# Attention scores in 64x32 tiles of the array, with another layout of queries, values and weight conversion

## The chip, the cores and the metric

One core of a Trainium2 chip runs the whole program. The metric is device time in microseconds (us) of one execution, as the median of several runs. The engines are PE (TensorE: matmuls and transposes), DVE (VectorE), ACT (ScalarE), POOL (GpSimd) and SP (SyncE, which here issues all DMAs); 16 DMA engines move the data.

## The reference

Three stages follow one another. The attention has 4 batches, 8 heads, 512 local and 32 global positions and a head dimension of 64. Global queries see all 544 keys; a local query sees the 32 global keys and the local keys at a distance of at most 32. Then come two FFNs on 2176 tokens with 512 features and 2048 hidden units; all is float32.

```python
s_g = scale * q_g @ concat(k_g, k_l).T            ; out_g = softmax(s_g) @ concat(v_g, v_l)
s_l = scale * concat(q_l @ k_g.T, masked(q_l @ k_l.T, |i-j| <= 32)); out_l = softmax(s_l) @ concat(v_g, v_l)
x   = concat(out_g, out_l) as [2176, 512]
x   = relu(x @ w_in)**2 @ w_out                    # first FFN
y   = rational(x @ w_in2) @ w_out2                 # second FFN, P/Q with coefficients a, b
```

The four weight matrices arrive with 8 bytes an element and are converted on the chip to float32; for the matmuls of the FFNs each is split into a high and a low part.

## The kernel before, in words

**Attention.** The work goes by quads: a quad is one batch and four heads, eight quads in all, and a quad has five groups: four local groups of 128 queries (four blocks of 32) and one global group (g = 4). In a software pipeline (the loop at L747, 41 iterations) iteration i does the scores of group i+3 (`do_S`, L589), the exponentials of group i+2, the transposes of the probabilities of group i+1 (`do_T`, L649), the product with the values of group i (`do_PV`, L679) and the transposes of group i-2's results into `xT` (`do_xT`, L713). All engines issue in the order of the program text: it is a hand-written order, with semaphores put in by the framework. Where group i+2 is global, the scores of group i+3, the first of the next quad, are placed late, after `do_xT` (L772).

For the scores of a block of 32 queries, L602 multiplies a stationary matrix of 128 rows (two heads of 64 features) and 64 columns (the queries of one head, zeros, and the other way round: `qbd`, a block-diagonal layout) by 128 keys of a window (32 global, 96 local). Two such matmuls (four heads) fill the 128 partitions of a bank; a group has eight. They go to one bank of PSUM from tag "S", which has two buffers. DVE adds the mask, takes the minimum and so the row's maximum (L608), ACT takes the exponentials (L616). PV (L696) has 16 matmuls of 128 rows and 32 columns a group.

`prep` (L548) transposes the queries and keys of later quads: keys two quads ahead, queries one. For the keys, the 32 global ones are copied by DVE into six slots (L556). For the queries, four transposes of [128, 128] a pass and four copies by ACT (L577) that sort them into the block-diagonal layout. Two passes a quad.

The values of a quad stand in 14 windows of 128 rows (32 global, 96 local), of three kinds by where the global rows lie: A, B and C, interleaved in memory. `load_v(n, "A")` (part 0) loads the local rows of the five A windows and the global rows of one; `load_v(n, "B")` makes the rest by seven DMAs inside SBUF (L458 to L465). All DMAs stand in SP's one queue. The tuples `LD` and `LD0` say in which group of a quad which load is issued, `PZ` and `PZ0` in which group which pass of `prep` runs.

**Weight conversion.** `todo` is a list of items, half weight tiles (16 feature tiles f, a half each for w_in and w_out). `cv_tick` advances them: every third tick loads one item, and later ticks run its steps on ACT (L121, L131), DVE (L124, L135, L139), POOL (L129, L144) and for the ready value a copy and a subtraction (L153, L159). An item marked spill is instead written back to DRAM as float32 and loaded later, ready ("f32"), when only the last two steps remain. In attention there are 63 ticks (3 in the first iteration, then 2 and 1 in turn), so 21 items: 14 for f = 0 to 6, four spilled for f = 14 and 15, three more. The first FFN group (`step`, L356, for the first 16 k) runs 14 ticks in three steps for the rest, before the weights of each f are needed.

**FFNs.** `step(k)` does twelve matmuls into "S" for one f (L252) and twelve for the output of an earlier one (L328), with the squares and splits on ACT and DVE between them (L265 to L276).

## Time and profile before

| | |
|---|---|
| runs | 969.3, 967.54, 963.17 us; median 967.54 |
| profiled execution | 964.78 us, of which the profile's span is 963.0 |
| busy, share of the span | PE 96%, PEld (weight loads) 87%, DVE 75%, ACT 59%, POOL 38% |
| DMA | 81.82 MB; queue of SP 32.3% of 16 engines |

A profile shows, for one execution, when each engine ran which instruction, and for each idle time which event ended it. The share over the whole span is a mean over stages with different limits. In a timeline a row is start, duration, engine, line, operation, tiles and, in brackets, the idle time before it and what ended it. PE's durations overlap, as matmuls are pipelined: the time of a group is read from its start to the start of the next. The granted clock is 1.00 at 2.4 GHz and 0.50 at 1.2 GHz.

### The profile page before, as it was taken

The page shows a single profiled execution, that of the slowest core. Times are in us where ns is not written, and L with a number is a line of the kernel's source. Part 1 is how long each engine was busy: PE and PEld are TensorE (multiplying, and loading weights), DVE is VectorE, ACT ScalarE, POOL GpSimd, SP SyncE. Part 2 cuts the span into 40 slices and gives each one's busy share as a digit, 9 for nine tenths or more (in the row PEclk, how much of TensorE's full clock was granted, in tenths as well). Part 3 has the DMA queues.
Part 4 walks back from the last instruction along what each step waited for, and adds up shares of the span by engine and source line. Part 5 has one row for each costly group of instructions (what it writes and reads, how often), then busy time and mean ns, then how long its engine had stood idle before and what let it go on. Part 6 is the DMA issues. An engine that isn't in the chain of part 4 may idle for free.

```text
span 963.0 us, 18278 instructions
## 1 busy us (share of the span) xinstructions
PE 920.3 (96%) x6794; PEld 833.4 (87%) x6794; DVE 719.5 (75%) x1525; ACT 572.8 (59%) x1223; POOL 366.8 (38%) x349
## 2 busy tenths in 40 slices
PE   8899988999999999999999988899999999999996
PEld 5677766989999999999999977789989989989874
DVE  4586768798645674453334599999999999999996
ACT  4697877678434553443324476666766666666674
POOL 2143433343211221111000088755555555555553
PEclk9899999999999999999999999999999999999999
DMA  9899998355522433222002322000010010010000
GB/s 216 175 231 243 211 210 210 99 152 167 155 90 92 148 116 114 95 88 77 1 1 66 99 66 74 3 30 4 1 33 1 1 33 1 1 33 1 8 27 22
DMA packets 78121, 81.82 MB, mean 85 GB/s; under 512 B 24528, under 2 KB 64720, under 8 KB 78032
## 3 DMA queue, kind: packets, MB, share of 16 engines
q1 hardware_dynamic: 78032, 80.66, 32.3%
q8 instruction: 53, 0.87, 0.4%
q14 instruction: 36, 0.29, 0.1%
HBM read 56.36 MB, written 13.89 MB: 73 GB/s over the span
## 4 chain that ended last, share of the span: by engine, by line
PE 57%; issue 13%; DVE 12%; POOL 6%; DMA 5%; ACT 4%; SPq 2%; POOLq 0%; DVEq 0%; ACTq 0%
PE S L252 26%; PE T L328 5%; PE PV L331 5%; PE tr L331 4%; PE T L331 4%; PE PV L328 4%; PE tr L328 3%; DMA S<-in_moe_w_in_dram 3%; POOL w L159 2%; POOL big L308 2%; DVE ts L300 2%; PE S L602 2%; DVE w L159 1%; POOL tq L289 1%; DVE T L139 1%
## 5 line engine op out<-in xcount | busy, mean ns | idle before, releaser
L252 PE MATMUL S<-big,w 128*128 128x384 f32 (+1 forms) x2304 | 410.3, 327 | 0.9 <-ACT big L265 0.9
L252 PEld LDWEIGHTS S<-big,w 128*128 128x128 f32 x2304 | 385.9, 188 | 9.7 <-ACT big L265 1.2
L144 POOL TENSOR_TENSOR T<-T,S 128x512 uint32<-128x512 uint32 x64 | 87.5, 1367 | 292.4 <-DVE T L139 184.2
L289 POOL TENSOR_TENSOR tq<-tq,big 128x384 f32<-128x384 f32 (+1 forms) x96 | 93.4, 973 | 261.4 <-DVE tq L287 249.4
L273 DVE TENSOR_TENSOR big<-big 128x384 f32<-128x384 f32 (+1 forms) x80 | 46.4, 580 | 141.8 <-ACT big L269 141.6
L308 POOL TENSOR_TENSOR big<-ts,big 128x384 fp32r<-128x384 f32 (+1 forms) x96 | 124.5, 1297 | 5.2 <-issue 1.9
L300 DVE SCALAR_TENSOR_TENSOR ts<-ts,coef,big 128x384 f32<-128x384 f32 (+1 forms) x96 | 125.6, 1308 | 0.0
L265 ACT ACTIVATE big<-S 128x384 f32<-128x384 f32 (+1 forms) x96 | 45.4, 473 | 114.1 <-PE S L252 112.5
L286 ACT ACTIVATE big<-S 128x384 f32<-128x384 f32 (+1 forms) x96 | 45.5, 474 | 105.2 <-PE S L252 78.9
L331 PE MATMUL PV<-w,big 128*128 128x512 f32 x288 | 99.9, 401 | 3.7 <-ACT big L307 2.6
L331 PE MATMUL T<-w,big 128*128 128x512 f32 x288 | 84.1, 400 | 11.5 <-POOL big L308 10.8
L328 PE MATMUL T<-big,w 128*128 128x384 f32 x384 | 88.0, 337 | 2.0 <-DVE big L276 1.8
L269 ACT ACTIVATE big<-big 128x384 fp32r<-128x384 f32 (+1 forms) x96 | 48.8, 508 | 64.4 <-PE T L328 27.0
L328 PE MATMUL PV<-big,w 128*128 128x384 f32 (+1 forms) x384 | 82.2, 322 | 0.3 <-DVE xs L707 0.3
L328 PE MATMUL tr<-big,w 128*128 128x384 f32 (+1 forms) x384 | 82.0, 322 | 0.0
L288 ACT ACTIVATE ts<-S,coef 128x384 f32<-128x384 f32 (+1 forms) x96 | 62.7, 653 | 25.7 <-POOL big L308 25.0
L331 PEld LDWEIGHTS T<-w,big 128*128 128x128 f32 x288 | 52.0, 188 | 25.4 <-POOL big L308 17.5
L331 PE MATMUL tr<-w,big 128*128 128x512 f32 x240 | 71.5, 395 | 0.0
L328 PEld LDWEIGHTS T<-big,w 128*128 128x128 f32 x384 | 68.1, 188 | 3.9 <-DVE big L276 3.9
L331 PEld LDWEIGHTS PV<-w,big 128*128 128x128 f32 x288 | 52.5, 188 | 19.4 <-POOL big L308 7.5
L328 PEld LDWEIGHTS PV<-big,w 128*128 128x128 f32 x384 | 64.9, 188 | 0.6 <-issue 0.6
L328 PEld LDWEIGHTS tr<-big,w 128*128 128x128 f32 x384 | 64.8, 188 | 0.0
(137 smaller groups left out, 1430.2 us busy)
## 6 DMA issues: line engine op xcount, KB each, us to landing
S<-in_moe_w_out_dram SPq DMA_DIRECT2D x32, 512.0 KB, 4.0
scr<-T SPq DMA_DIRECT2D x36, 256.0 KB, 2.2
T<-scr SPq DMA_DIRECT2D x36, 256.0 KB, 2.7
S<-in_moe_w_in_dram SPq DMA_DIRECT2D x32, 256.0 KB, 5.5
S<-in_moe_w_in_dram SPq DMA_DIRECT2D x16, 512.0 KB, 3.9
out_dram<-xT SPq DMA_DIRECT2D x17, 256.0 KB, 2.6
kr<-in_k_l_dram SPq DMA_DIRECT2D x7, 512.0 KB, 8.2
qr<-in_q_l_dram SPq DMA_DIRECT2D x7, 512.0 KB, 6.1
```

Of the source, the lines that this page charges most:

```text
L144: gp.tensor_tensor(out=u, in0=u, in1=it["S"][:, :, 0], op=ALU.add)
L252: pe.matmul(h, wk[k][s], x[k][t], start=m == 0, stop=m == 3 * NK - 1)
L265: sc.activation(g, h, AF.Relu)
L269: sc.activation(hi, g, AF.Square)
L273: ve.tensor_tensor(out=g, in0=g, in1=g, op=ALU.mult)
L286: sc.activation(av, h, AF.Abs)
L288: sc.activation(s, h, AF.Identity, scale=coef[:, 3:4], bias=coef[:, 2:3])
L289: gp.tensor_tensor(out=q, in0=q, in1=av, op=ALU.mult)
L300: ve.scalar_tensor_tensor(out=s, in0=s, scalar=coef[:, 0:1], in1=r, op0=ALU.add, op1=ALU.mult)
L308: gp.tensor_tensor(out=lo, in0=s, in1=hi.bitcast(F32), op=ALU.subtract)
L328: pe.matmul(y[m][:, 0:n], a, x, start=st and z == 0, stop=sp and z == 2)
L331: pe.matmul(y[m], a, x, start=st and z == 0, stop=sp and z == 2)
```

## The change

Scores: a group's 16 matmuls now have 64 rows (one head) and 32 columns (one block); even heads of a pair go to one bank, odd ones to another, so a group takes two banks of "S". Each bank holds two blocks of two heads side by side, and the masks are made for pairs of blocks. Queries: a new `turn_q` has ACT copy a quad's raw queries from [head, c, d] to [c, head, d], after which four transposes a pass give two heads' queries by one copy; there are no zeros to set. Values: the windows of one kind lie side by side in memory (`win`); the global rows are loaded three times and spread by POOL; four DMAs inside SBUF remain. The global keys' slots are filled by POOL instead of DVE. The copy of the transposed probabilities of g = 3 goes from ACT to DVE. The loads of q and k move in `LD`. Weights: no items are spilled in attention; 14 items are loaded there, three more in the last five groups.

```diff
-    SPL = (14, 15)
     if wide:
-        todo += items(0, range(NPRE), "wide")
-        todo += items(0, SPL, "wide", True)
-        for f in range(NPRE, NF):
-            todo += items(0, (f,), "f32" if f in SPL else "wide")
+        todo += items(0, range(NF), "wide")
         todo += items(1, range(NF), "wide", True)
...
     todo.reverse()
+    later = len(todo) - 2 * NPRE
...
+        def win(x):
+            return 5 * (x % 3) + x // 3
...
-            A, Bw, C = wf[:, 0::3], wf[:, 1::3], wf[:, 2::3]
+            A, Bw, C = wf[:, 0:5], wf[:, 5:10], wf[:, 10:14]
...
-                sy.dma_start(w[96:128, 0, :, 0:D], vg)
+                for p, a in ((96, 0), (64, 5), (32, 10)):
+                    sy.dma_start(w[p:p + 32, a, :, 0:D], vg)
                 return
             sy.dma_start(Bw[0:64], A[32:96])
             sy.dma_start(Bw[96:128, 0:4], A[0:32, 1:5])
             sy.dma_start(C[0:32], A[64:96, 0:4])
             sy.dma_start(C[64:128], A[0:64, 1:5])
-            g = wf[96:128, 0:1]
-            sy.dma_start(A[96:128, 1:5], g.to_broadcast([32, 4, 4 * (D + 1)]))
-            sy.dma_start(Bw[64:96], g.to_broadcast([32, 5, 4 * (D + 1)]))
-            sy.dma_start(C[32:64], g.to_broadcast([32, 4, 4 * (D + 1)]))
+            for p, t, m in ((96, A, 4), (64, Bw, 4), (32, C, 3)):
+                gp.tensor_copy(t[p:p + 32, 1:], t[p:p + 32, 0:1].to_broadcast([32, m, 4 * (D + 1)]))
...
-        for t in qbd[0] + qbd[1] + qgbd:
+        for t in qgbd:
             ve.memset(t[0:64, :, 1], 0.0)
             ve.memset(t[64:128, :, 0], 0.0)
...
+        def turn_q(n):
+            qs[n] = raw.tile([128, 4, 4, D], F32, tag="qs", name="qs")
+            sc.copy(qs[n], qraw[n].rearrange("p h c d -> p c h d"))
...
-                ve.tensor_copy(t[:, :, 0:32], kgt[2 * hq + p][:, b:b + 1, :].to_broadcast([128, 6, 32]))
+                gp.tensor_copy(t[:, :, 0:32], kgt[2 * hq + p][:, b:b + 1, :].to_broadcast([128, 6, 32]))
...
-                for h in range(2):
-                    for c in range(2):
-                        o = 256 * h + 128 * c
-                        pe.transpose(pt[:, o:o + 128], src[:, 2 * p + h, 2 * c:2 * c + 2, :].rearrange("p c d -> p (c d)"), ident)
-                for h in range(2):
-                    for z in range(2):
-                        o = qbd[n % 2][p][64 * h:64 * h + 64, :, h].rearrange("r b (e c z) -> r b e c z", c=2, z=2)
-                        i = pt[64 * z:64 * z + 64, 256 * h:256 * h + 256].rearrange("r (c b e) -> r b e c", c=2, e=8)
-                        sc.copy(o[:, :, :, :, z], i)
+                for c in range(4):
+                    pe.transpose(pt[:, 128 * c:128 * c + 128],
+                                 src[:, c, 2 * p:2 * p + 2].rearrange("p h d -> p (h d)"), ident)
+                sc.copy(qt[n % 2][p].rearrange("r (e c) -> r e c", c=4), pt.rearrange("r (c e) -> r e c", c=4))
...
-                sp = bank("S")
+                sp = [bank("S"), bank("S")]
                 s = ssp.tile([128, 4, 128], F32, tag="s", name="s")
-                for u in range(4):
-                    bl = 4 * g + u
-                    o = 32 * win_of(bl)
-                    for p in range(2):
-                        pe.matmul(sp[64 * p:64 * p + 64, 128 * u:128 * u + 128],
-                                  qbd[n % 2][p][:, bl].rearrange("r a q -> r (a q)"),
-                                  kt[p][:, o:o + 128], start=True, stop=True)
+                for j in range(2):
+                    for h in range(4):
+                        for v in range(2):
+                            p, i2 = divmod(h, 2)
+                            r, c, bl = slice(64 * i2, 64 * i2 + 64), 32 * (v + 2 * p), 4 * g + 2 * j + v
+                            o = 32 * win_of(bl)
+                            pe.matmul(sp[i2][c:c + 32, 128 * j:128 * j + 128], qt[n % 2][p][r, 32 * bl:32 * bl + 32],
+                                      kt[p][r, o:o + 128], start=True, stop=True)
                 def lows(us):
                     for u in us:
-                        ve.tensor_tensor_reduce(out=s[:, u], in0=sp[:, 128 * u:128 * u + 128],
-                                                in1=mskf[:, mask_of(4 * g + u)], scale=-0.125, scalar=3.0e38,
+                        i2, j = divmod(u, 2)
+                        ve.tensor_tensor_reduce(out=s[:, u], in0=sp[i2][:, 128 * j:128 * j + 128],
+                                                in1=mskf[:, MSK[2 * g + j]], scale=-0.125, scalar=3.0e38,
                                                 op0=ALU.add, op1=ALU.min, accum_out=nmx[:, u:u + 1])
...
-                (sc.copy if g in (0, 3) else ve.tensor_copy)(t.rearrange("p u c -> p (u c)"), tp)
+                (sc.copy if g == 0 else ve.tensor_copy)(t.rearrange("p u c -> p (u c)"), tp)
...
+        turn_q(0)
         for i in (2, 3, 0, 1):
             prep(0, i)
...
-        LD = ("k", "A", "q", "B", "")
-        LD0 = ("k", "A", "B", "q", "")
+        LD = ("q", "A", "", "B", "k")
+        LD0 = ("kq", "A", "", "B", "k")
+        TQ, TQ0 = ((), (), (), (), (2,)), ((), (1,), (), (), (2,))
...
-                    if n + 2 < 2 * B:
-                        load_qk(n + 2, "qk".index(c))
+                    m = n + 2 + (c == "k" and g == 4)
+                    if m < 2 * B:
+                        load_qk(m, "qk".index(c))
...
+            for dn in (TQ0 if n == 0 else TQ)[g] if i < NS else ():
+                if n + dn < 2 * B:
+                    turn_q(n + dn)
...
             for _ in range(1 + i % 2 if i else 3):
-                cv_tick(0)
+                cv_tick(later - 3 * (i >= NS - 5))
```

The new masks take 36 selects on POOL instead of 32, ahead of the first loads in POOL's order, and PV picks its rows and windows by the new layouts.

## Rows read from the trace of the kernel before

**Rows 1.** The page, part 2: DMA busy in tenths, 40 slices of the span.
```profile
DMA  9899998355522433222002322000010010010000
```

**Rows 2.** Windows: busy us of each engine, instructions, granted clock, DMA share, GB/s.
```profile
core 0: us, PE busy (x) PEld busy (x) DVE busy (x) ACT busy (x) POOL busy (x), PEclk, DMA share, GB/s
14.00:168.00 154.00, 138.13 (x2425) 106.86 (x2426) 106.70 (x501) 117.39 (x324) 53.60 (x51) 0.96 1.00 214
...
200.00:225.00 25.00, 22.11 (x119) 20.20 (x118) 23.69 (x33) 16.74 (x33) 10.35 (x7) 1.00 0.47 135
```

**Rows 3.** Timeline of PE, 92 to 112 us.
```profile
92.42 1.09 PE L602 MATMUL S<-kt,big 128*64 128x128 f32 x16 [0.66 <-ACT sg L641]
93.44 0.66 PE L696 MATMUL PV<-vw,pt 128*32 128x65 f32 x32
94.03 1.09 PE L602 MATMUL S<-kt,big 128*64 128x128 f32 x16
...
98.45 1.09 PE L602 MATMUL S<-kt,big 128*64 128x128 f32 x16
99.47 0.65 PE L655 MATMUL T<-ident,s 128*128 128x128 f32 x4
```

**Rows 4.** Timeline of PE, 28 to 42 us.
```profile
32.65 0.43 PE L602 MATMUL S<-kt,qbd 128*64 128x128 f32 x2 [1.11 <-ACT qbd L577]
34.19 1.97 PE L602 MATMUL S<-kt,qbd 128*64 128x128 f32 x14 [1.11 <-ACT qbd L577]
...
37.11 1.98 PE L602 MATMUL S<-kt,qbd 128*64 128x128 f32 x16
```

**Rows 5.** Waits, 14 to 168 us: total us, times, longest.
```profile
ACT T L121 <- DMA S<-in_moe_w_in_dram: 9.4, 4, 5.6
ACT T L121 <- DMA S<-in_moe_w_out_dram: 4.4, 2, 2.9
```

**Rows 6.** Timeline of DVE, 92 to 112 us.
```profile
93.56 0.29 DVE L608 CUSTOM_DVE_ANT_0 s<-S,msk 128x128 f32<-128x128 f32 x1 [3.07 <-PE S L602]
...
94.41 0.42 DVE L124 TENSOR_SCALAR T<-T 128x512 f32<-128x512 f32 x1
```

**Rows 7.** Groups of instructions, 14 to 168 us: busy, mean ns, idle before.
```profile
L129 POOL TENSOR_SCALAR S<-S 128x512 uint32<-128x512 uint32 x19 | 12.7, 669 | 29.6 <-DMA S<-in_moe_w_in_dram 24.6 <-DMA S<-in_moe_w_out_dram 3.9
L577 ACT COPY qbd<-tr 64x256 f32<-64x256 f32 x32 | 12.2, 382 | 1.3 <-PE tr L572 0.9
...
L657 ACT COPY pt<-T 128x512 f32<-128x512 f32 x16 | 9.5, 592 | 1.6 <-PE T L655 1.4
...
L556 DVE COPY kt<-kgt 128x192 f32<-128x192 f32 x14 | 5.9, 420 | 0.0
...
L641 ACT ACTIVATE sg<-S,nmx 128x384 f32<-128x384 f32 x8 | 4.7, 584 | 0.5 <-PE T L672 0.4
...
L642 ACT ACTIVATE sg<-S,nmx 128x160 f32<-128x160 f32 x8 | 3.1, 391 | 0.0
```

**Rows 8.** DMA view, 0 to 160 us: packets; issues with KB, us to landing.
```profile
DMA packets 47002, 34.59 MB, mean 216 GB/s; under 512 B 22309, under 2 KB 45587, under 8 KB 46974
...
big<-in_v_g_dram SPq DMA_DIRECT2D x4, 32.0 KB, 3.5
```

**Rows 9.** Timeline of all engines, 0 to 45 us.
```profile
8.28 0.44 SPq L456 DMA_DIRECT2D big<-in_v_g_dram  x1
...
13.97 0.43 PE L602 MATMUL S<-kt,big 128*64 128x128 f32 x2 [0.82 <-ACT big L577]
```

**Rows 10.** Timeline of DVE, the first FFN group.
```profile
203.30 0.41 DVE L135 TENSOR_SCALAR T<-T 128x512 uint32<-128x512 uint32 x1
...
204.96 1.54 DVE L124 TENSOR_SCALAR T<-T 128x512 f32<-128x512 f32 x1
```

**Rows 11.** Timeline of PE, the first FFN group.
```profile
199.74 2.24 PE L252 MATMUL S<-big,w 128*128 128x384 f32 x12
...
225.21 2.24 PE L252 MATMUL S<-big,w 128*128 128x384 f32 x12
...
229.37 2.24 PE L252 MATMUL S<-big,w 128*128 128x384 f32 x12
```

More of the change, by code (lines that the diff above doesn't have):

```diff
@@ L470 @@
         make_identity(nc, ident)
+        msk = cst.tile([128, 5, 4, 32], F32, name="msk")
+        gp.memset(msk, 0.0)
+        kinds = [3] + [b % 3 for b in range(NB - 2)] + [4]
+        pairs = [tuple(kinds[b:b + 2]) for b in range(0, NB, 2)]
+        some = list(dict.fromkeys(pairs))
+        MSK = [some.index(x) for x in pairs]
+        for i, pair in enumerate(some):
+            for h in range(4):
+                p, m = slice(32 * h, 32 * h + 32), pair[h % 2]
+                for low, c in ((True, (0, 0, 0, None, 1)[m]), (False, (2, 3, 3, 1, None)[m])):
+                    if c is not None:
+                        gp.affine_select(out=msk[p, i, c], in_=msk[p, i, c], pattern=[[1 if low else -1, 32]], base=0,
+                                         channel_multiplier=-1 if low else 1, compare_op=ALU.is_ge, fill=NEG)
+                if m > 2:
+                    gp.memset(msk[p, i, (2, 0)[m - 3]], NEG)
+        mskf = msk.rearrange("p i c k -> p i (c k)")
         big1, big2 = big(1), big(2)
-        qbd = [[(big1, big2)[p][:, 0:1024].rearrange("r (b a q) -> r b a q", a=2, q=32) for p in range(2)],
-               [cst.tile([128, NB, 2, 32], F32, name=f"qbd1{p}") for p in range(2)]]
+        qt = [[(big1, big2)[p][:, 0:SL] for p in range(2)],
+              [cst.tile([128, SL], F32, name=f"qt1{p}") for p in range(2)]]
         qgbd = [cst.tile([128, B, 2, 32], F32, name=f"qgbd{p}") for p in range(4)]
@@ L551, in prep @@
             isk, p = divmod(i, 2)
[L552 removed]
+            src = kraw[n] if isk else qs[n]
             if isk:
@@ L695, in do_PV @@
                     for h in range(4):
-                        pe.matmul(pv[32 * h:32 * h + 32, u], t[u][:, 32 * h:32 * h + 32],
-                                  w[:, min(max(4 * g + u, 1), NB - 2) - 1, h, :], start=True, stop=True)
+                        c = 32 * (u % 2 + 2 * (h // 2))
+                        pe.matmul(pv[32 * h:32 * h + 32, u], t[2 * (h % 2) + u // 2][:, c:c + 32],
+                                  w[:, win(min(max(4 * g + u, 1), NB - 2) - 1), h, :], start=True, stop=True)
             else:
@@ L701, in do_PV @@
                         pe.matmul(pv[32 * h:32 * h + 32, 0], t[u][0:rows, 32 * h:32 * h + 32],
-                                  w[0:rows, wi, h, :], start=u == 0, stop=u == len(GCH) - 1)
+                                  w[0:rows, win(wi), h, :], start=u == 0, stop=u == len(GCH) - 1)
             sm = sml.tile([128, 4], F32, tag="sm", name="sm")
```

27 lines of the change are left out of this document (4 added, 23 removed).

## The prediction

> **What bounds the kernel now.** I read the slices of the page first: the DMA row is at nine tenths or more over the first sixth of the span, which is the attention [rows 1]. Then the windows: from 14 to 168 us, attention from its first scores to the first step of the first FFN, PE is busy 138.1 of 154 us at a mean granted clock of 0.96, DMA at a share of 1.00, DVE 106.7, ACT 117.4, POOL 53.6 [rows 2]. So two things are full there, PE and the DMA engines. PE's time holds 154 - 138.1 = 15.9 us idle; a mean clock of 0.96 means about a twelfth of the stretch at the lower level, some 12 us, of which half, 6 us, is excess. That makes 22 us that are not PE's proper work, and 132 us that are: eight quads of 16.5 us.
>
> Then PE's timeline of one quad, to see what a start-to-start distance is. One group's scores (16 instructions) run from 98.45 to 99.47, 1.02 us; one PV (32 instructions of 32 columns, four column strips at once) from 93.44 to 94.03, 0.59 us [rows 3]. The idle times before them name ACT: 0.66 us for the exponentials of the global group (L641) [rows 3], 1.11 us for the query copies (L577), after which the same scores take 1.98 us, because the clock has dropped [rows 4]. The waits say why ACT is late: apart from its own work it stands 9.4 + 4.4 us in front of weights that DMA has not landed [rows 5]. Last, the first FFN group, 200 to 225 us: DVE is busy 23.7 of 25 us and PE loses 2.9 [rows 2].
>
> **The change part by part.** The sum is made against the profiled execution's own 964.8 us (span 963.0), which is 2.8 below the median of the runs.
>
> *Scores.* Before, 8 matmuls of 64 columns per group, two at once: four rounds in 1.02 us [rows 3]. After, 16 matmuls of 64 rows and 32 columns; the eight of one half group have eight different places in the array (two row halves, four column strips), so two rounds if all run at once: 0.51 us. If row halves do not run side by side, four at once give four rounds again, 1.02 us. No row of before has two row halves. PV has the same 32 instructions in 0.59 us [rows 3]; I take 0.60, nearest to it. 32 groups x 0.42 = 13.4 us off PE's path; bounds 0 and 32 x 0.51 = 16.3.
> By the Trainium skill (TensorE: Matmul & The Clock Gate, Part 3: Packing small matmuls) row and column strips compose, sixteen small tiles having run over ten times as fast as one after another; by it the gain would be the upper bound, 16.3. No run here shows it yet.
>
> *Banks.* A group's scores now fill both buffers of "S". The next group's first pair of matmuls needs both banks, so it waits until all four reductions of the group before are done (0.21 us each: 93.56 to 94.41, 0.85 us [rows 6]). In most iterations PE has over 3 us of transposes and PV in between (95.05, where 94.03's scores end, to 98.45 [rows 3]), which hides it. Not where the scores of a quad's first group are placed late: there only one PV (0.59 us) stands between 92.42's scores and 94.03's [rows 3]. Wait: 0.12 until DVE starts, 0.85, less 0.59, about 0.4 us, in seven quads. The first group also waits for both exponentials of the global group, not one: L642 after L641, 0.39 us more [rows 7] where that wait exists, say half the quads. Together +4 us; bounds 0 and 8 x 0.8 = 6.4. Behind the waiting matmul stand PV and the next transposes; DVE and ACT wait for those.
>
> *Queries.* Eight copies of 0.38 us a quad (L577) go, 3.05 us; a turning copy of 128x1024 comes, 1.13 us by the slope between L641 and L642 (224 columns in 0.193 us), and two copies of 0.59 us like L657's [rows 7]: 2.31 us. ACT also hands one 0.59 us copy a quad to DVE. PE's transposes stay four a pass. ACT thus gains 1.3 us a quad, and the blocks of four copies, 1.5 us, that hold back scores and the exponentials of the global group shrink to 0.6. The turn stands at the end of a quad, one to two groups ahead of the transposes that read it, so nothing waits for it but the exponentials behind it on ACT, which have a group's time.
>
> *Value tiles.* The window copies go from 1248 pieces of 1040 bytes a quad to 192 longer ones (64 + 32 + 32 + 64 rows, each one joined run), or to 832 if each 1040 bytes stays a packet; 256 pieces of 256 bytes come for the two more loads of v_g. Of the 47,002 packets of the first 160 us [rows 8] some 10,000 are such pieces. SP issues 13 value DMAs a quad instead of 14. Four weight halves fewer are loaded and written back in this stage (63 ticks make 21 items before, 14 + 3 after). DMA falls below full, so ACT's 13.8 us of waiting for weights [rows 5] mostly goes. The moved loads (q from the third group of a quad to its first, k from the first to the last of the quad before) give each a longer lead; they pass on SP only value loads and weights. In the first quad k(3) stands in the group that still transposes k(2), so SP waits there for PE, a group at most, with one weight load behind it that ACT and POOL need three ticks later: nothing, or 1 us once if that cover fails.
>
> *What term two is worth.* Of the 22 us of idle and slow clock I take back 10: the stall and slow clock after 32.65 (2.2 us idle, and about 3 at half clock: 0.9 in each of two groups of scores, the rest in what lies between [rows 4]), the query stalls and the weight waits of later quads. Bounds: 0 if DMA stays full, 18 if only the exponential waits remain. What is late next is DVE: its work per quad hardly falls (key copies of 0.42 us twice go to POOL [rows 7], one such copy as ACT hands over comes), while the quad shrinks from 19 us (154 / 8) to about 17.
>
> *POOL.* It gets three value copies of up to 1040 elements a quad and two key copies of 192. At L129's 1.3 ns an element [rows 7] that is 3.7 + 0.5 us a quad, beside 6.7 now (53.6 / 8); at half or double that rate 2.1 or 8.4. The masks, now ahead of them, take four more selects, under 1 us at the start. Consumers are a group or more away, so I cost them nothing, except at the start: POOL does the three copies of v(0), which wait for v_g (issued at 8.28 [rows 9], 3.5 us to landing [rows 8], two more loads behind it), before the first key copies that every score needs. Landing near 12, 3.7 us of copies, 0.5 of key copies: the first scores can start near 16.2 instead of near 14, but then run without the query copies between them. I take +1.5; bounds -2 and +3.
> An instruction of the kind L124 is 0.42 us at 94.41 [rows 6] and 1.54 us at 204.96 [rows 10]. The Trainium skill (SBUF — State Buffer, Who interferes with whom) says that the port VectorE's fast copies share with GpSimd is an exclusive lock, the later one waiting for the whole of the other's instruction. By it each POOL copy can cost DVE up to 1.1 us where a conversion meets it; the sum would rise by what of that reaches PE.
>
> *No weights set aside.* Four halves (f = 14, 15) come in the first FFN group as full conversions, not as ready values. Before, they cost DVE there only the last subtraction; now also clamp, shift and sign, 1.46 us, and 1.1 us of the blocked kind [rows 10]. In that group DVE sets the pace: five steps from 199.74 to 225.21 take 5.09 us each, and 4.16 once the ready values come (225.21 to 229.37) [rows 11]. Four halves at 14/9 a step hold the slow pace for 2.6 steps longer: 2.6 x 0.93 = 2.4 us. At worst all 4 x 2.56 = 10.2 us reach PE. I take 4, nearer the step rows. ACT (two more passes a half, 16.7 of 25 us busy) and POOL (one addition, 10.4 of 25) have room [rows 2].
>
> *Sum:* -13.4 - 10 + 4 + 1.5 + 4 = -13.9: 950.9 on the profiled execution's scale, 953.6 on that of the median, 967.5.
>
> **The rivals.**
> A. The row halves do not run side by side. For: no row shows it. Against: column strips do, in PV. Scores stay at 1.02 us: -0.5 us, 967.0. Chance 0.14.
> B. DVE takes the bound through the banks: DVE, 69% loaded now (106.7 / 154 [rows 2]) and some 75% after, does the four reductions so late that scores wait in every group, not in one a quad. For: both banks are held by one group. Against: DVE sat idle 3.07 us before such reductions [rows 6], and 3.4 us of other PE work lies in between in most iterations. Break-even is (13.9 + 4) / 32 = 0.56 us a group; at 1 us a group the total is 32 - 17.9 = 14 us up, 981.6. Chance 0.08.
> C. Conversion in the first FFN group costs the full 10.2: 959.8. For: DVE there is at 95%. Chance 0.10.
> D. DMA stays as full as it is (runs not joined, 256-byte pieces added), and the second term gives nothing: -3.9, 963.6. Chance 0.09.
> E. All of it comes: 16.3 + 18, banks 4, start 0, conversion 2.4: -27.9, 939.6. Chance 0.09.
>
> **How the numbers follow.** The forecast has 0.50. Its own range is 946 to 961: with scores at 0.51 and a second term of 14 it is 946.7, with a second term of 5 and conversion at 6 it is 960.6. 80% must reach to A and D on the upper side and part of E below: 943 to 967. About 1% (10 us) is what a measurement of this kernel tells from no change, so faster means under 958. Of the forecast's 0.50 about 0.46 lies there, all of E, some of C and D: 0.63; A, most of C and D and the rest: 0.28; B: 0.09.
>
> **What would show it.** Right: scores of a group near 0.6 us start to start; a wait of scores for reductions once a quad; no clock drop after 30 us; ACT's waits for weights gone; the first FFN step near 150 us rather than 168; steps of some 5.1 us up to f = 15. Wrong: scores at 1.02 (A), scores waiting for DVE in all groups (B), a DMA share still at 1.0 with waits for weights (D). The forecast as a whole is wrong if the attention ends less than 10 us earlier.

## The result: slower by about 1%, with no gain in the attention

The changed kernel took 979.82 us (median of 4 runs, 975.54 to 982.25) beside 965.69 for the kernel before: a ratio of 1.0127 with a 95% interval from 1.0088 to 1.0167. Measured a second time, beside other runs of before, it was 972.04 us (8 runs, 966.56 to 977.72) and a ratio of 1.0054 (1.0018 to 1.009). So it is slower, by 0.2 to 1.7%, where 1.4% less had been forecast. The profiled execution took 978.73 us, its span 976.9. Single runs that lie over 1.5% above the fastest of their kernel are left out of the medians and ratios here, as one of e6_four_banks at 980.14 us.

Windows of the kernel after; the columns are those of [rows 2], and its first and second rows answer to the two there:
```profile
core 0: us, PE busy (x) PEld busy (x) DVE busy (x) ACT busy (x) POOL busy (x), PEclk, DMA share, GB/s
14.00:168.00 154.00, 134.75 (x2896) 97.44 (x2896) 107.34 (x479) 100.97 (x271) 76.17 (x82) 0.90 0.75 179
200.00:225.00 25.00, 23.09 (x129) 22.12 (x127) 24.59 (x34) 18.51 (x35) 10.60 (x8) 1.00 0.58 160
225.00:250.00 25.00, 18.92 (x93) 17.34 (x92) 24.17 (x33) 19.55 (x39) 10.81 (x8) 0.93 0.53 157
```
Most of what the change set out to remove is gone: the DMA share of the attention fell from 1.00 to 0.75, ACT's work from 117 to 101 us. But the granted clock of PE is 0.90 instead of 0.96 (0.93 in the second profile of the kernel after), PE's idle time 154 - 134.75 = 19.3 us instead of 15.9, and the first FFN matmul starts at 169.7 us; before it was 167.8. In the third row DVE is busy 24.2 of 25 us, and PE has lost 6.

Timeline of PE after, three stretches [rows 3]; a matmul counts as two instructions, so a group is x32:
```profile
66.44 0.66 PE L602 MATMUL S<-kt,big 64*32 64x128 f32 x31
69.47 0.27 PE L602 MATMUL S<-kt,big 64*32 64x128 f32 x1 [2.37 <-issue]
...
94.19 1.07 PE L602 MATMUL S<-kt,big 64*32 64x128 f32 x32
95.20 0.66 PE L697 MATMUL PV<-vw,pt 128*32 128x65 f32 x32
95.98 1.08 PE L602 MATMUL S<-kt,big 64*32 64x128 f32 x32
96.99 0.63 PE L568 MATMUL tr<-ident,kr 128*64 128x128 f32 x4
...
100.38 0.67 PE L602 MATMUL S<-kt,big 64*32 64x128 f32 x32
100.98 0.66 PE L655 MATMUL T<-ident,s 128*128 128x128 f32 x4
```
A group left alone takes 0.60 us, start to start (100.38 to 100.98): the two row halves and four column strips do run side by side. But the groups at 94.19 and 95.98 take 1.01, as before the change, for two reasons. In the group at 95.98 nothing starts for 0.28 us ahead of the first matmul into the second bank, which stands behind a semaphore: a wait for that bank. In the group at 94.19 nothing starts for 0.28 us either, but in mid-group, from 94.55 to 94.83, where no instruction waits for a semaphore. The rows show next to no idle time for either, since matmuls overlap and the earlier ones are still ending. Of the 32 groups, 11 stand in PE's timeline as one row of 0.67 to 0.76 us; the rest are longer, or broken in two, as at 66.44. By the starts of the instructions, 12 pause ahead of the second bank, and four pause in mid-group without a semaphore, as the one at 94.19 does.

The same by groups of instructions, 14 to 172 us, first the two rows of local scores of the kernel before, then of the kernel after (busy us, mean ns of one, idle time ahead of them and its releasers):
```profile
L602 PE MATMUL S<-kt,qbd 128*64 128x128 f32 x256 | 20.0, 296 | 2.9 <-ACT qbd L577 2.2 <-ACT sg L641 0.7
L602 PE MATMUL S<-kt,big 128*64 128x128 f32 x256 | 19.2, 296 | 3.4 <-ACT big L577 1.9 <-ACT sg L641 1.3
```
```profile
L602 PE MATMUL S<-kt,big 64*32 64x128 f32 x512 | 16.3, 311 | 9.1 <-issue 2.8 <-POOL kt L558 2.4 <-ACT sg L641 1.9
L602 PE MATMUL S<-kt,qt 64*32 64x128 f32 x512 | 14.9, 289 | 4.6 <-DVE nmx L608 2.6 <-DVE T L135 0.9 <-ACT sg L641 0.7
```
These four rows are the whole case in small. With their waits the scores took PE 20.0 + 2.9 + 19.2 + 3.4 = 45.5 us before and 16.3 + 9.1 + 14.9 + 4.6 = 44.9 after. Thirty-two groups at 0.60 us would be 19.2; the rest is waiting, part of it inside the rows, and the lower clock: at 0.50 the group at 24.06 takes 1.04 us without a pause.

PE's waits after, 10 to 172 us (total, times, longest), the longest lines and all that are put down to issue:
```profile
PE S L602 <- DVE nmx L608: 4.3, 6, 1.4
PE S L602 <- issue: 2.8, 2, 2.4
PE S L602 <- ACT sg L641: 2.6, 2, 1.9
PE S L602 <- POOL kt L558: 2.4, 1, 2.4
PE tr L571 <- issue: 2.1, 1, 2.1
PE T L655 <- issue: 1.7, 2, 1.4
PE PV L702 <- issue: 1.4, 1, 1.4
```
There are three kinds: waits for a bank (reductions, and the exponentials of the global group), 7 us; the start, where the first scores wait for POOL; and 8 us for which the profile shows no cause.

In the first FFN group, 165 to 250 us, the longest wait of PE was before and is after:
```profile
PE T L328 <- DVE big L276: 1.8, 3, 1.0
```
```profile
PE T L325 <- DVE big L273: 7.4, 7, 2.5
```
From the first FFN matmul to the 384th, sixteen steps' worth, it is 74.1 us before and 81.8 after, by the starts of the matmuls in the two traces.

### The profile page after: what moved, and what is told of

Read it like the earlier page. It is cut to its first block, busy times and chain, and to the rows that moved or that the text cites. A ratio compares the mean times of both kernels' runs of the same rounds, so it can differ in the third digit from the quotient of the medians.

```text
span 976.9 us, 19308 instructions
## 1 busy us (share of the span) xinstructions
PE 926.6 (95%) x7306; PEld 832.7 (85%) x7306; DVE 727.4 (74%) x1509; ACT 563.5 (58%) x1179; POOL 399.0 (41%) x391
## 4 chain that ended last, share of the span: by engine, by line
PE 59%; issue 15%; DVE 14%; POOL 6%; ACT 3%; DMA 2%; SPq 1%; POOLq 0%; DVEq 0%; ACTq 0%
PE S L249 25%; PE PV L328 4%; PE tr L328 4%; PE T L328 4%; PE T L325 4%; PE tr L325 3%; PE PV L325 3%; PE S L602 2%; POOL big L305 2%; POOL w L159 2%; DVE ts L297 2%; DVE T L124 2%; DVE w L159 2%; DVE T L139 1%; PE T L655 1%
## 5 line engine op out<-in xcount | busy, mean ns | idle before, releaser
L249 PE MATMUL S<-big,w 128*128 128x384 f32 (+1 forms) x2304 | 414.9, 329 | 0.6 <-DVE w L159 0.6
L249 PEld LDWEIGHTS S<-big,w 128*128 128x128 f32 x2304 | 390.1, 188 | 9.4 <-DVE w L159 0.9
L283 ACT ACTIVATE big<-S 128x384 f32<-128x384 f32 (+1 forms) x96 | 45.5, 474 | 105.2 <-PE S L249 79.0
```

The costliest lines, as they stand in the source:

```text
L249: pe.matmul(h, wk[k][s], x[k][t], start=m == 0, stop=m == 3 * NK - 1)
L283: sc.activation(av, h, AF.Abs)
```

## The experiments

All are timed beside runs of the kernel before. "First FFN step" is the start of the first FFN matmul in the run's trace, "16 steps" the time from it to the 384th.

| run | median us (runs) | ratio to before, 95% | first FFN step | 16 steps |
|---|---|---|---|---|
| before | 965.69 (4) | 1 | 167.8 | 74.1 |
| before_again | 966.0 (10) | 1.0007 (0.9971, 1.0042) | 169.2 | 74.3 |
| after | 979.82 (4) | 1.0127 (1.0088, 1.0167) | 169.7 | 81.8 |
| after_again | 972.04 (8) | 1.0054 (1.0018, 1.009) | 167.2 | 81.7 |
| e1_set_aside | 969.27 (10) | 1.0019 (0.9982, 1.0055) | 172.2 | 73.9 |
| e2_scores_only | 968.46 (10) | 0.9991 (0.996, 1.0021) | 171.2 | 73.8 |
| e3_old_scores | 963.81 (10) | 0.9952 (0.9923, 0.9981) | 162.5 | 82.1 |
| e4_values_only | 958.41 (4) | 0.9896 (0.9839, 0.9953) | 162.1 | 74.6 |
| e5_more_code | 969.88 (10) | 1.0016 (0.9983, 1.005) | 171.6 | 74.1 |
| e6_four_banks | 966.23 (9) | 0.9998 (0.9961, 1.0035) | 165.6 | 73.9 |
| e7_halves_in_turn | 964.86 (10) | 0.9969 (0.994, 0.9998) | 168.8 | 74.1 |
| e8_own_t_bank | 981.61 (4) | 1.0172 (1.0122, 1.0221) | 181.3 | 78.0 |
| e9_bank_act_start | 983.94 (4) | 1.0192 (1.0122, 1.0261) | 182.4 | 76.1 |
| e10_copy_on_act | 975.09 (4) | 1.0111 (1.0066, 1.0155) | 176.0 | 73.9 |
| e11_cheap_scores | 967.1 (10) | 0.9999 (0.9966, 1.0031) | 170.8 | 73.8 |
| e12_cheap_values | 955.21 (9) | 0.9884 (0.9848, 0.9921) | 158.3 | 74.4 |

**Which part costs: four kernels with parts of the change.** e1 is the changed kernel with f = 14 and 15 set aside again:
```diff
-        todo += items(0, range(NF), "wide")
+        todo += items(0, range(NPRE), "wide")
+        todo += items(0, SPL, "wide", True)
...
-                cv_tick(later - 3 * (i >= NS - 5))
+                cv_tick(0)
```


> The changed kernel with only its last part undone: weights for f = 14 and 15 are set aside in attention again. Theory (conversion): the first FFN group takes 72 us again and not 80, attention grows by 0 to 2 us, the total falls by 6 to 8 us against the changed kernel, to about 973. Rival (the loss lies in attention alone): the total stays within 2 us of 980.

e2 is the kernel before with the new scores, masks, queries and their loads, and the copy that goes from ACT to DVE; values, key copies and weights stay as before.

> The kernel before with only the scores in 64x32 tiles, the turned queries, their masks and the new order of the q and k loads; values, global keys and weights as before. Theory (PE's instructions come in blocks of 256 and are loaded too late when the scores issue twice as many in less time): idle of PE put down to issue stays, 8 us or more in pieces over 0.5 us, the first FFN step comes at 163 to 170 us, the total is 962 to 970. Rival (the small tiles are a gain that the values on POOL and the weights take away): no such idle, first FFN step at 150 to 157 us, total 948 to 955.

e3 is the changed kernel with scores and queries as before.

> The changed kernel with scores and queries as before, so with the new values, the global keys on POOL and no weights set aside. Theory (late instructions): no idle of PE put down to issue over 0.5 us, attention shorter than before by 5 to 10 us because DMA is relieved, the first FFN group 7 us longer; total 960 to 967. Rival (POOL's copies and the key copies behind them cost the time): first FFN step at 168 us or later, total 972 or more.

e4 is the kernel before with the value tiles by kind, POOL's copies of the global rows and the masks made first.

> The kernel before with only the value tiles of one kind side by side, spread by POOL (masks made first); scores, queries, global keys and weights as before. Theory (late instructions hurt the scores; the values are a gain): DMA share in attention falls from 1.0 to 0.85 or less, first FFN step 5 to 10 us earlier than 168, total 955 to 961. Rival (values cost time through POOL): total 966 or more.

Measured: e1 is 10.5 us under the changed kernel's first measurement and 2.8 under its second; its sixteen steps are back at 73.9, but its attention ends 2.5 to 5 us later than in the two profiles of the changed kernel, where no more than 2 had been expected. e3, which differs from e4 by the conversions and by POOL's key copies, has 82.1 against e4's 74.6, and 5.4 us more in the median. So the conversions cost 7.5 us in the first group. The value part is a gain of 1.0% (0.5 to 1.6): its first FFN step is 6 to 7 us earlier, its DMA share 0.86. The score part gains nothing on the old values (e2), and on the new values it loses: from e4 to e1 the first FFN step goes from 162.1 to 172.2, the time from 0.9896 to 1.0019 of before. Between these two POOL's key copies come in as well; in e3 they move the first FFN step by 0.4 us only. What I expected of e2, at least 8 us put down to issue, was a miss: it has 0.4 us of that. It waits for the exponentials of the global group (5.6 us) and for ACT's turn of the queries (5.1) instead.

**Late code?** Six stalls of PE in the first profile of the changed kernel are put down to issue, and four in its second. All ten stand at the 194th of a block of 256 instructions, in PE's own order. The page's DMA part counts the instruction queue at
```profile
q8 instruction: 53, 0.87, 0.4%
```
packets and MB before, and after at
```profile
q8 instruction: 57, 0.93, 0.4%
```
Two more, of 0.28 us, stand at that place inside score rows without showing as idle time: the pause at 94.55 and one at 135.32. That speaks for pieces of code that arrive late. e5 gives the kernel before more PE instructions and little else:
```diff
+                for u in range(2):
+                    for h in range(4):
+                        pe.matmul(pvb[32 * h:32 * h + 32, u, 80:84], t[u][:, 32 * h:32 * h + 32],
+                                  w[:, 0, h, 0:4], start=True, stop=True)
```


> The kernel before, with eight more matmuls of 4 columns in every local group's PV, written to bank columns that nothing reads: 32 more PE instructions a group, as the new scores bring, with no more waits and almost no more PE time. Theory 'late code' (PE's longer instruction stream is fetched too late behind the attention's other transfers, which the changed kernel shows as 8 us of waits put down to issue): such waits of 0.5 to 2.5 us appear here too, 5 to 8 us in all, and the time rises by 8 to 12 us, to 975 to 980. Rival (more instructions cost only their own issue, at most 0.15 us a group): no wait put down to issue above 0.5 us, time up by 0 to 5 us, 967 to 973.

Waits of e5, 10 to 172 us:
```profile
PE PV L697 <- issue: 2.8, 2, 1.8
...
PE S L602 <- issue: 1.9, 1, 1.9
...
PE PV L706 <- issue: 1.2, 2, 1.0
...
PE S L627 <- issue: 0.2, 1, 0.2
```
The stalls came, 6.1 us in all, those over half a microsecond again at the 194th of 256; the waits of neither profile of before have one. So the added instructions brought them here. Their number alone does not decide: e9 below has as many PE instructions as the changed kernel (7306 matmuls in the profile) and no such stall, e3 has the old number (6794) and two, of 0.9 and 0.4 us, where I had expected none over 0.5. In e5 they did not cost the 8 to 12 us that was feared: the first FFN step is 2.3 to 3.8 us later than in the two profiles of before, the ratio 1.0016 with an interval on both sides of 1. In the two profiles of the changed kernel they make 8.0 and 5.6 us, and the first FFN step comes at 169.7 and 167.2, so some of them seem to reach it. That the cause is the loading of code is argued from the place and from the instruction queue, not shown.

**Banks.** PSUM's eight banks go by tags, two each: S for scores, T for transposes of the exponentials, PV for the products with the values, tr for the other transposes. e6 has four banks for scores instead of two; the transposes of the exponentials share the two banks of tr:
```diff
-                sp = [bank("S"), bank("S")]
+                sp = [bank("ST"[i % 2]) for z in range(2)]
...
-                s0, s1 = bank("S"), bank("S")
+                s0, s1 = bank("ST"[i % 2]), bank("ST"[i % 2])
...
-                tp = bank("T")
+                tp = bank("tr")
```


> The changed kernel with four weight halves set aside as before (the one that took 969.3 us), and four banks for scores in place of two: groups take the pair S and the pair T in turn, and the transposes of the exponentials go to the two tr banks. Theory 'banks' (a group that holds both banks makes the next one wait for reductions and for both global exponentials, and each stall of PE is followed by a stretch at the lower clock): waits of scores for sg and nmx in the attention fall from some 9 us to under 3, the mean granted clock from 14 to 168 us rises from 0.91 to 0.95 or more, and the time falls by 6 to 12 us, to 957 to 963. Rival 'DVE and ACT are simply late' (their queues set the pace, whichever buffer shows it): the waits move to T, tr and PV, the time stays within 966 to 972.

e7 keeps two banks and fills one after the other:
```diff
-                for j in range(2):
-                    for h in range(4):
-                        for v in range(2):
-                            p, i2 = divmod(h, 2)
+                for i2 in range(2):
+                    for j in range(2):
+                        for p, v in ((0, 0), (0, 1), (1, 0), (1, 1)):
```


> The same kernel of 969.3 us with the 16 score tiles of a group in another order: first the eight of one row half (one bank), then the eight of the other (the other bank). Then only four tiles run side by side, and the second bank is needed half a group later. Theory 'PE's own work' (what counts is that eight tiles run together): a group's scores take about 1.0 us instead of 0.6, and the time rises by 8 to 13 us, to 977 to 982. Theory 'banks' (PE's gain is lost in waits for the second bank anyway): scores take 1.0 us, the waits for nmx and sg shrink by about as much, and the time stays within 964 to 973.

Of e6 the score rows by groups of instructions, 14 to 172 us:
```profile
L605 PE MATMUL S<-kt,big 64*32 64x128 f32 x256 | 6.5, 293 | 2.6 <-POOL kt L561 2.5
L605 PE MATMUL T<-kt,qt 64*32 64x128 f32 x256 | 6.4, 294 | 0.7 <-ACT sg L644 0.5 <-issue 0.2
L605 PE MATMUL T<-kt,big 64*32 64x128 f32 x256 | 5.8, 282 | 0.0
L605 PE MATMUL S<-kt,qt 64*32 64x128 f32 x256 | 5.3, 275 | 0.0
```
its window of the attention:
```profile
14.00:168.00 154.00, 127.74 (x2950) 91.73 (x2951) 116.29 (x499) 103.77 (x277) 84.39 (x92) 0.98 0.84 199
```
and PE's longest waits:
```profile
PE tr L726 <- DVE pt L660: 9.9, 11, 1.4
PE tr L574 <- ACT qs L551: 6.6, 6, 4.1
```
Here the scores with their waits are 27.3 us. In e1, which differs by the banks alone, the same sum is 43.6 (15.0 + 8.8 + 14.5 + 5.3), 16.3 more: 8.2 are waits for reductions and for the exponentials of the global group, 5.5 are longer busy rows, 2.6 are put down to issue. So the two banks cost the scores up to 14 us, about what the new tiles save (32 x 0.42 = 13.4). The granted clock is 0.98 here, and 0.91 in e1. But only 6.6 us reach the first FFN step, and 3.0 the median. PE's idle time is 26 us now, in front of the transposes: some 14 us for copies out of the tr banks by DVE and ACT, 6.6 for ACT's turn of the queries (qs). Both theories were half right: the waits of scores and the clock are those of "banks", the waits at tr and the time those of the rival. e7 missed its number for a group (a row is 0.69 to 1.50 us, most often 0.77, since the second half starts before the first is done), but points the same way as e6: with eight tiles of one bank ahead of the other's, the median is 4.4 us under that of e1, with intervals that overlap a little.

**Who is late?** Three kernels share the banks out again, or move one copy.
```diff
-        return ps.tile([128, 512], F32, tag=tag, name=tag)
+        return ps.tile([128, 512], F32, tag=tag, name=tag, bufs=1 if tag in ("T", "PV") else 2)
...
-    ytags = itertools.cycle(("T", "T", "PV", "PV", "tr", "tr"))
+    ytags = itertools.cycle(("X", "X", "T", "PV", "tr", "tr"))
...
-                sp = [bank("S"), bank("S")]
+                sp = [bank("SX"[i % 2]) for z in range(2)]
```


> The kernel with four banks for scores, which took 966.8 us, with the other four shared out anew: two for tr, one for the transposes of the exponentials (T), one for PV. There the transposes of the outputs had waited 9.9 us for copies of the exponentials out of the shared tr banks. Theory 'banks' (what is left of PE's idle time is again a matter of banks): those waits go, PV waits no more than 2 us for its one bank, the first FFN step comes 4 to 8 us earlier than 165.6, the time is 959 to 963. Rival 'DVE is late' (its queue carries 116 of 154 us, and whoever needs DVE waits): the same us are waited for T or PV instead, the time stays within 964 to 969.

e9 adds the first two lines of this to e8, e10 only the first to e6:
```diff
-                (sc.copy if g == 0 else ve.tensor_copy)(t.rearrange("p u c -> p (u c)"), tp)
+                (sc.copy if g in (0, 3) else ve.tensor_copy)(t.rearrange("p u c -> p (u c)"), tp)
...
-                gp.tensor_copy(t[:, :, 0:32], kgt[2 * hq + p][:, b:b + 1, :].to_broadcast([128, 6, 32]))
+                (gp if n else ve).tensor_copy(t[:, :, 0:32], kgt[2 * hq + p][:, b:b + 1, :].to_broadcast([128, 6, 32]))
```


> The kernel with T and PV banks of their own and two further edits: ACT keeps the copy of the fourth group's exponentials (0.69 us a quad off DVE, 0.59 onto ACT), and in the first quad DVE does the key copies, which POOL did only after the three value copies (scores then start near 14 us, not 15.5). Theory 'DVE is late': 4 to 6 us less than the kernel with those banks, since 5.5 us of DVE's queue go and 1.5 at the start. Rival 'banks alone': 1.5 us less, from the start only.

> The kernel with four banks for scores, which took 966.8 us, with one edit: ACT keeps the copy of the fourth group's exponentials, as before the change. Theory 'DVE is late': 3 to 6 us less, 961 to 964, with the waits for pt down from 12 us to under 8. Rival 'ACT is as late as DVE' (the copy only changes its queue): 965 to 969.

Waits of PE in e8, 10 to 172 us:
```profile
PE T L675 <- DVE pt L671: 11.9, 8, 2.9
PE PV L700 <- DVE xs L711: 8.0, 7, 2.1
PE PV L705 <- DVE xs L711: 5.7, 4, 2.6
```
All three are slower, against what I expected of each. With one bank for T and one for PV, PE waits 25.6 us for DVE to empty them (e8): neither tag can do with one bank. A copy handed back from DVE to ACT costs 8.9 us in the median (e10 against e6). Waits for the copies of the exponentials do fall there, from 12.2 us to 7.3, as "DVE is late" had it, but waits for ACT's key copies rise from under 1 us to 8, and 5.5 us are put down to issue against 1.9 in e6. So ACT is no better a place for this copy; how much of the loss is the copy and how much the stalls stays open. In e9 the third group's scores end 2.6 us earlier than in e8 (15.77 for 18.41) and DVE is busy 7 us less, and neither reaches the time.

**Was PE's score time on the path at all?** e11 and e12 write keys and queries as bfloat16, so PE does the same score matmuls in less time, in the same order, with the same banks and semaphores: e11 in the kernel before, e12 in e4.
```diff
-                t = ktp.tile([128, 6, 128], F32, tag=f"kt{p}", name=f"kt{p}")
+                t = ktp.tile([128, 6, 128], BF, tag=f"kt{p}", name=f"kt{p}")
...
-        qgbd = [cst.tile([128, B, 2, 32], F32, name=f"qgbd{p}") for p in range(4)]
+        qgbd = [cst.tile([128, B, 2, 32], BF, name=f"qgbd{p}") for p in range(4)]
```


> The kernel before with the scores' operands (keys, queries, global queries) written as bfloat16 by the same copies: the score matmuls are the same in number, order, banks and waits, but take PE a fraction of their time (an estimate: some 0.3 us a group instead of 1.02). Only their precision changes. Theory 'PE's score time is on the path': 0.7 us x 32 = 22 us less PE work, so the first FFN step comes 12 to 22 us earlier than 167.8 to 169.2 and the time falls to 946 to 956. Rival 'the chain of handovers binds' (PE, DVE and ACT wait for each other through two banks each; PE done sooner only waits longer, and its clock falls with it): the first FFN step within 5 us of before, PE's idle time up by 15 us or its clock down, the time 963 to 970. Rival 'DMA binds' gives the same for this kernel, and is told apart by the next.

> The same bfloat16 operands in the kernel that has the new value tiles alone (958.4 us), where the DMA share is 0.86 instead of 1.00. Theory 'PE's score time is on the path': first FFN step at 142 to 152 instead of 162, 938 to 948 us. Rival 'handovers': within 5 us of 162, 954 to 960. Rival 'DMA binds before, PE here': no gain in the kernel before, 10 us or more here.

Score rows of e11, as above:
```profile
L603 PE MATMUL S<-kt,qbd 128*64 128x128 bf16 x128 | 8.2, 257 | 3.5 <-ACT qbd L578 2.8 <-ACT sg L642 0.7
L603 PE MATMUL S<-kt,big 128*64 128x128 bf16 x127 | 7.1, 241 | 4.1 <-ACT sg L642 1.6 <-ACT big L578 1.5 <-DVE nmx L609 0.9
```
and its window:
```profile
14.00:168.00 154.00, 122.93 (x2063) 91.91 (x2063) 102.88 (x493) 116.54 (x318) 53.36 (x51) 0.86 0.99 210
```
The window of e12:
```profile
14.00:168.00 154.00, 125.77 (x2218) 96.55 (x2219) 118.18 (x516) 124.64 (x334) 80.03 (x77) 0.92 0.84 200
```
What PE waits for in e11, 10 to 172 us, the longest lines:
```profile
PE tr L567 <- ACT qbd L578: 6.2, 2, 3.6
PE S L603 <- ACT qbd L578: 2.8, 2, 1.5
PE PV L697 <- DMA vw<-vw: 2.8, 1, 2.8
PE S L624 <- ACT sg L642: 2.6, 1, 2.6
```
In e11 a group's scores take 0.34 us at the full clock, the scores with their waits shrink from 45.5 to 22.9 us, and nothing comes of it: the first FFN step at 170.8, the ratio 0.9999. PE is busy 123 instead of 138 us, its clock 0.86 instead of 0.96; the idle time stands in front of ACT's copies of the queries, the exponentials and, with 5.5 us, DMAs. With DMA relieved (e12) the first FFN step comes 3.9 us earlier than in e4, of the 23 us that these rows save there (45.3 to 22.3). "Handovers" had forecast within 5 us of 162 and 954 to 960 us. So in the kernel before, PE's time for scores is not on the path, and with the new values about a sixth of it is, by one pair of profiles. A lower clock gives part of PE's saving back in e11, but it is not the whole reason: in e6 the clock is 0.98, PE is busy 10 us less than before, and its first FFN step comes only 2 to 4 us earlier than in the two profiles of before.

**Twice the same kernel.** Both kernels were profiled again, unchanged, since PE's unbroken first FFN showed two spacings.

> The kernel before, unchanged, for a second profile. In the first FFN, where PE never waits, the profiles so far show one of two even spacings of 384-column matmuls at the same granted clock of 1.00: 0.1733 us (before, and the two kernels with the old scores) and 0.1767 (the changed kernel, and the two with the new scores), 4.8 us over the stage. Theory 'phase' (which of the two it is comes from the last stall ahead of the unbroken stretch, not from the kernel): this kernel's runs lie in two clusters some 5 us apart, and the profile may show either spacing, with PE records from 400 to 500 us near 579 or near 567. Theory 'kernel' (the new scores bring the slower spacing): 0.1733 here, and one cluster.

> The changed kernel once more, unchanged, for more runs and a second profile. If its loss against the kernel before is the conversion in the first FFN group (7.6 us longer in the profiles) and an attention that ends no earlier, and not the two spacings of the first FFN, its runs fall in two clusters as well, and the median is 7 to 10 us above that of before: 973 to 978. If the slower spacing belongs to it, there is one cluster, 979 to 983.

Windows of 400 to 500 us of the kernel before, its second profile, the kernel after and its second profile:
```profile
400.00:500.00 100.00, 100.00 (x579) 100.00 (x578) 42.74 (x79) 36.35 (x72) 8.05 (x6) 1.00 0.16 51
```
```profile
400.00:500.00 100.00, 100.00 (x568) 100.00 (x567) 42.83 (x79) 36.07 (x71) 9.36 (x7) 1.00 0.16 51
```
```profile
400.00:500.00 100.00, 100.00 (x567) 100.00 (x567) 42.40 (x78) 36.02 (x70) 10.75 (x8) 1.00 0.18 59
```
```profile
400.00:500.00 100.00, 100.00 (x579) 100.00 (x578) 43.53 (x80) 36.66 (x73) 9.36 (x7) 1.00 0.17 54
```
Either kernel shows either spacing, 579 or some 567 matmuls in 100 us at the same granted clock of 1.00; the runs of before_again lie at 962.7 to 966.6 (six) and 970.2 to 974.1 (four). The theory "kernel" fell. The eight runs of after_again spread from 966.6 to 977.7 without two clusters, and their median is under the 973 to 978 that I expected. Profiles can so be compared in pairs of one spacing: after less before_again, both with the slower, is 978.73 - 971.74 = 7.0 us; after_again less before, both with the faster, is 970.95 - 964.78 = 6.2. The sixteen steps make 7.5 of that in either pair, and the first FFN step is 0.5 us later in the one and 0.6 earlier in the other. So by place the whole loss is the conversions in the first FFN group, and the attention takes as long as before. Setting the four halves aside again saves less than that 7.5, since the attention then ends later: 978.73 - 973.82 = 4.9 us from after to e1, both with the slower spacing. The profiled executions of the first measurement differ by 14 us because before had the faster spacing there and after the slower.

## Why the prediction was wrong, by its own steps

**What bounds the kernel: the step that failed.** "Two things are full there, PE and the DMA engines" and "132 us that are" PE's proper work took PE's busy share for the path. e11 halves PE's score work and the attention does not shorten; PE's idle time grows instead, by 15 us. PE stands in a ring: scores wait for DVE to empty banks (4.3 us after), DVE's reductions for scores (32.8 us before), ACT for DVE's minima (4.2 us before, 7.5 after), PE's transposes for ACT and DVE (21 us in e6). PE done sooner waits longer. In the changed kernel and in e11 the granted clock was lower too (0.96 to 0.90 and 0.86), which fills the row "PE busy" again; that is not so whenever PE idles, as e6 has 26 us idle at 0.98. A busy share of 0.9 was no proof of a bound. Of the two things called full, the other did pay: with the value tiles alone (e4) the DMA share falls to 0.86 and the first FFN step comes 6 to 7 us earlier.

**Scores.** The size of one was right: 0.60 us a group, so rival A is out. The sum of -13.4 was not: with their waits, 45.5 became 44.9. That eight tiles on two row halves run at once agrees with the packing rule of the Trainium skill that the prediction quotes.

**Banks: the term that was mis-sized.** I gave it 4 us and an upper bound of 6.4, since "in most iterations PE has over 3 us" of other work between. At the place that I named, the second group of a quad, the wait is near the 0.4 us that I had: 0.12 ahead of the row at 95.98 and 0.41 of stretch in it, 0.5 to 0.6 in five of the seven quads. But five more groups pause ahead of the second bank, and the exponentials of the global group hold scores for up to 1.9 us (2.6 in the second profile) where I had 0.39 more. Measured, the scores' rows with their waits are 16.3 us longer with two banks than with four (e1 against e6), up to 14 of it by the banks; 6.6 reach the first FFN step. Rival B, which I held unlikely at 0.08, has the right engine and banks, but scores pause for the second bank in 12 groups of 32 and not in all. That its end point of 981.6 lies near the measured 979.82 is luck: by place the loss is conversion, and part of the difference of the runs is spacing. The Trainium skill (PSUM — Partial Sum Buffer, PSUM bank collisions raise a hardware error) says that matmuls of different row tiles may not write one bank at a time; by it the second bank is the price of row halves and can't be saved by placing. No run here shows that rule.

**Second term, -10.** Not there: idle time rose by 3.4 us, and the clock fell. Its premise did come, so rival D is out: the DMA share went to 0.75. ACT's waits for weights fell less than "mostly goes": 2.5 + 6.1 us remain of 13.8 [rows 5]. The drop of the clock behind 32.65 did go. In its place the clock is at 0.50 from 17.1 to 27.3 us (before: 16.4 to 19.9) and behind some of the later stalls, as from 105.8 to 112.6, where one of 2.14 us ends at 106.77; behind the one of 2.37 us that ends at 69.47 it stays at 1.00.

**Start, +1.5: right.** The third group's scores end at 21.18 instead of 19.94 us, 1.2 later. In POOL's timeline after:
```profile
12.15 3.05 POOL L465 COPY big<-big 32x1040 f32<-32x1040 f32 x3 [2.26 <-DMA big<-in_v_g_dram]
15.26 1.21 POOL L558 COPY kt<-kgt 128x192 f32<-128x192 f32 x4
```
The three value copies take 3.05 us (estimate: 3.7), and the first scores start at 15.66.

**Conversion, +4: mis-sized, 7.5.** The slow pace of DVE was slower than 5.09 us a step: from 206.34 to 239.70 PE's scores of a step come every 5.56 us, and these six steps take 33.4 us where before they took 29.3 (204.24 to 233.53). The step behind them takes 9.9 us instead of 6.5. Rival C named 10.2; the truth lies between.

**Queries, values, POOL.** ACT's work fell by 16.4 us; 12.3 of that are the queries and the copy handed to DVE, for which 10.6 was forecast, eight times 1.33. Most of the rest is fewer weights (L121 10.3 us instead of 13.6). That nothing waits for the turn of the queries was wrong: PE's transposes wait 0.9 us for it in the changed kernel, 2.2 in its second profile, 6.6 in e6. The values part alone, 958.41 us, was worth about what the second term was to bring, which is a coincidence; in profiles of one spacing it is 5.5 us (959.33 against 964.78). POOL's new copies take 32.6 us, as forecast (33.6); its work in the window grew by 22.6 only (76.2 - 53.6), as it had fewer weights to convert. The price of POOL beside DVE is there too: DVE's step L139 takes 693 ns on average before and 886 after, L135 427 and 739. After the change, the 7 of 14 L135 that ran beside a POOL instruction took 1.05 us, the other 7 0.43, as all do before. That agrees with the rule of the Trainium skill on the shared port that the prediction quotes; I had charged nothing for it.

So the sum -13.4 - 10 + 4 + 1.5 + 4 should have read about 0 for scores, banks, second term and start together, since what the values give (e4) is what the new scores take again (e1), and 7.5 for the conversion: +6 to +7, as the pairs of one spacing show. Why the new scores take that much is shown in part only: four banks give back 6.6 us of the 10 at the first FFN step (e6), and e6 still stands 3.5 behind e4.

The range ended at 967, 5 us under the second measurement and 13 under the first: it took a gain on PE as certain in every case but B.

**A version that beats both.** e4, the value part alone, at 0.9896 (0.9839 to 0.9953) of before. With scores in bfloat16, which changes their precision, it is 955.21 us (e12).

## What to carry to other kernels

Before pricing PE time that a change saves, make that work cheap in the old kernel with nothing else moved (operands of a cheaper type will do): if the time stays, the engine is busy but not on the path. Look at the granted clock beside it, since a lower one gives part of the saving back. When a change doubles the banks that one step holds, price the wait for the slowest reader of each bank in every iteration, not by the work that lies between in the timeline of a faster order. Compare two profiles only when a long stage that neither changes runs at the same pace in both.

## What the runs showed that I had not expected

- An unbroken stream of 384-column matmuls keeps one of two spacings, 0.1733 or 0.1767 us, at the granted clock of 1.00. In the traces here it changes only where PE stalls, so the last stall ahead of the first FFN's long stretch seems to decide; what in it does is open. From the 384th to the 2304th FFN matmul it is 311.5 us in one profile of before and 316.6 in the other.
- PE stalls of 0.3 to 3 us without a releaser, all at one place in blocks of 256 PE instructions, most of them where 16 score tiles, or eight 4-column matmuls, stand in each group.
- A wait for a bank hides inside a busy row: the 16 matmuls of the group at 95.98 stretch from 0.60 to 1.01 us with no idle time shown. So does a stall without a releaser, at 94.19. Only the starts of the single instructions, and which of them stand behind a semaphore, tell the two apart.
